# A gated unit's down projection in seven block products for the second half of the tokens, with weight combinations made beside the up products and up sums kept in PSUM

## The chip, the cores and the metric

The kernel runs on one core of a Trainium2 chip. Its metric is the device time of one launch, in microseconds (us). Engines are named as in the profile: PE is TensorE's matmul and PEld its weight load, DVE is VectorE, ACT is ScalarE, POOL is GpSimd, SP is SyncE, which here only issues DMAs.

## The reference

Input is x of 2048 tokens by 640. A state-space convolution comes first and is untouched here; then comes a gated unit without nonlinearity:

```python
x = x + ga * _A_ref(h, ...)                  # state-space convolution, by FFT
h = _layernorm(x, axis=-1) * (1 + cb) + sb
g = einsum("bsd,df->bsf", h, w_gate)         # 2048 x 640 by 640 x 1536
u = einsum("bsd,df->bsf", h, w_up)
x = x + gb * einsum("bsf,fd->bsd", g * u, w_down)   # 2048 x 1536 by 1536 x 640
```

All data are fp32.

## The kernel before

The gated unit begins about 519 us into the program and runs in two halves of 1024 tokens. A half has two token blocks tb of 512. In each half an up stage makes h = g * u, transposed (features on partitions, 512 tokens on the free axis), and a down stage multiplies it with w_down and adds the residual.

Every factor of a matmul is split into hi and lo parts of type fp32r: `hilo` has ACT write a rounded copy and DVE subtract it from the original. A product is three matmuls: hi by hi, lo by hi, hi by lo. `prod` issues them for a list of blocks of the contraction axis.

**Up stage.** The features F = 1536 are NF = 12 blocks of 128; block i counts through both halves (0 to 23). Tokens (the two blocks of 512), the contraction axis and the pair of gate and up weights make a two by two block product, which is done by seven products of blocks for eight (Winograd's form), with the fifth 128 of the contraction axis apart. For each i: `sums_u` (POOL) builds weight differences in tf, `split_u` splits them into wth/wtl and wsuh/wsul, `split_g` splits the gate weights into wsgh/wsgl. `x_1` and `x_2` (15 matmuls of 512 columns) multiply the gate weights with the first tokens; `y_1`, `z_1`, `y_2`, `z_2`, `y_3` (39 matmuls) are the other products. Each of these seven products has a PSUM bank of its own, from six banks pa0 to pa5 in turn, and the partial sums are added in SBUF: S6, S67 and c by DVE, ZT and the final product by POOL. x_1 and x_2 run AHEAD = 4 blocks ahead. The token combinations (`s_sums`, `s_split`, `s_one`, `s_five`) stand at the start of a half.

**Down stage.** For each tb, `down(tb, f)` runs over the 12 blocks f, four groups t of 128 tokens, three hi/lo terms and two column pieces (C0 = 384 and the other 256 of the 640 columns). h is the stationary factor, w_down (already times gb; `fold` makes it in the first half, on POOL, and keeps it in DRAM as wdg) the moving one. `d_prep` splits one block of h and one of weights, LEAD = 3 blocks ahead. `fin` adds the residual and stores. During the first half's down stage the list `LATER` prepares the second half's tokens.

**Order and queues.** Each engine works off its instructions in the order in which the program emits them (`tc.manual_schedule`), so the loop at the end of the program is the schedule. All loads of this part are issued by SP, in program order: `raw` loads pairs of gate or down weights into wga (two buffers), `raw_u` gate and up weights into wgb and wur, `res_l` the residual rows.

Of the kernel before, what the change touches and what calls it, by code (L numbers as in the profile page):

```python
# [224 lines left out]
def tile_kernel(ctx: ExitStack, tc: tile.TileContext, I, out):  # L225
# [762 lines left out]
    LEFT = {"wga", "wgb", "wur", "xb0", "xb1", "hh1", "hl1", "a5", "a6", "a7", "a8", "a9", "wsgh", "wsgl", "e"}  # L988

    PAIRS = []  # L990
    for h in range(2):
        PAIRS += [("g", h * NF + 2 * p) for p in range(NF // 2)]
        PAIRS += [("d", 2 * h + T, 2 * p) for T in range(2) for p in range(NF // 2)]

    def raw():

        k = PAIRS.pop(0)
        t = mk("wga", [P, 2 * D], F32, 2)
        f = k[-1] % NF
# [8 lines left out]
        for j in range(2):  # L1008
            WR[(*k[:-1], k[-1] + j)] = w[j]
# [45 lines left out]
    def prod(ps, ks):  # L1055

        for n, (a, b) in enumerate(((0, 0), (1, 0), (0, 1))):
            for m, (w, k, x, l) in enumerate(ks):
                PE.matmul(ps, w[a][:, k], x[b][:, l], start=n == 0 and m == 0, stop=n == 2 and m == len(ks) - 1)  # L1059

    BANK = [0]

    def pa(j=None):

        if j is None:
            j = BANK[0]
            BANK[0] += 1
        return ps_a.tile([P, 512], F32, name=f"pa{j % 6}")

    def x_e(i):  # L1070
        UE[i] = mk("e", [P, 512], F32, 4)
        act(UE[i], UX.pop(i))

    def x_c(i):
        V.tensor_tensor(a_tile(i % NF), UX.pop(i), UE[i], op=OP.add)
# [25 lines left out]
    def head_st(tb):  # L1101
        if tb == 1:
            return a_tile(TV0 + NB - 1)[:, : 24 * NB].rearrange("p (i k s) -> p i k s", i=4, k=NB)
        return wp.tile([P, 4, NB, 6], F32, name="st0")
# [197 lines left out]
    for t in range(3 * NK + 24):  # L1302
# [17 lines left out]
        if t == 3 * NK + 1:  # L1320
# [3 lines left out]
            wp = ctx.enter_context(tc.tile_pool(name="wp", bufs=1, reuse_waits="tile"))  # L1324
            wdg = dram1.tile([P, NF, D], F32, name="wdg")
            wv = [I[n].rearrange("(k p) f -> p k f", p=P) for n in ("B_w_gate", "B_w_up", "B_w_down")]
# [19 lines left out]
    TMP = ("s6", "z", "s67")  # L1346
# [20 lines left out]
    def s_sums(k, E=G):  # L1367
# [3 lines left out]
        s4 = tmp(TMP[1 + k])  # L1371
# [20 lines left out]
    ZT, S6, S67 = {}, {}, {}  # L1392

    def y_1(i):
        ps = pa()
# [256 lines left out]
```

## Time and profile before

| | us |
|---|---|
| median of 3 runs | 1001.46 (999.91 to 1002.73) |
| the profiled execution | 1001.29 |
| its span, first to last instruction | 999.2 |
| PE busy in the span | 900.0 (90%) |
| DVE, POOL, ACT busy | 762.8, 564.3, 561.9 |

Busy time of PE is modelled from pipelined matmuls; the distance from one matmul to the next is shorter than the duration in a row. A row of a view by line or tile gives a name as output<-inputs; the helper `hilo` puts all its operations on two lines (L230 for ACT, L1024 for DVE), so they are told apart by tile. A wait in brackets is the idle time of the engine ahead of an instruction and what ended it.

### The profile page before, as it was taken

What the parts mean: (1) busy time and instruction counts of PE and PEld (TensorE: products, weight loads), DVE (VectorE), ACT (ScalarE), POOL (GpSimd) and SP (SyncE); (2) the same over time, 40 slices, a digit from 0 to 9 for tenths busy, and PEclk for the clock granted to TensorE, in tenths of its full rate; (3) what the DMA queues carried; (4) which work ended last, traced back from release to release, by engine and by line L of the source; (5) the groups of instructions that cost most, each with busy time, mean ns of one, the idle gap of its engine ahead of it and who ended that gap; (6) DMA issues with size and microseconds to landing.
All of it is one profiled execution on the core that took longest, in us unless ns stands there. A gap on an engine that the chain in (4) does not pass through costs nothing.

```text
span 999.2 us, 26832 instructions
## 1 busy us (share of the span) xinstructions
PE 900.0 (90%) x11192; PEld 727.2 (73%) x11192; DVE 762.8 (76%) x1399; ACT 561.9 (56%) x1048; POOL 564.3 (56%) x415
## 2 busy tenths in 40 slices
PE   4867898899789689998888999999999999999998
PEld 3565556675576467776555888879998888889998
DVE  8798569889979997975769788777576887768452
ACT  4869989987878979752354323235463422223331
POOL 5978899799789899930032667650112365542000
PEclk9877889999899899999999999999999999999999
DMA  8728754555256454577673442535635232212341
GB/s 265 254 50 301 227 176 135 194 163 167 68 163 202 129 161 120 164 248 214 210 210 123 153 150 87 184 132 159 209 134 202 88 105 80 79 53 59 100 159 53
DMA packets 147817, 153.16 MB, mean 153 GB/s; under 512 B 9200, under 2 KB 125424, under 8 KB 146288
## 3 DMA queue, kind: packets, MB, share of 16 engines
q1 hardware_dynamic: 145968, 148.43, 46.8%
q10 hardware_dynamic: 1728, 3.02, 0.8%
q8 instruction: 88, 1.44, 0.6%
q14 instruction: 33, 0.27, 0.1%
HBM read 110.45 MB, written 40.96 MB: 152 GB/s over the span
## 4 chain that ended last, share of the span: by engine, by line
PE 63%; DVE 16%; ACT 10%; issue 4%; DMA 4%; POOL 2%; SPq 1%; DVEq 0%; ACTq 0%; POOLq 0%
PE pa L1059 26%; PE pa L1463 16%; PE kg L807 2%; DMA xsb<-A_u 2%; PE kg L822 2%; PE psfc L889 2%; ACT L230 1%; PE psfb L889 1%; PE psfa L889 1%; PE psfc L946 1%; PE psfb L946 1%; PE psfa L946 1%; PE psfc L868 1%; ACT trb L230 1%; PE psfa L844 1%
## 5 line engine op out<-in xcount | busy, mean ns | idle before, releaser
L710 POOL TENSOR_TENSOR EQ<-LQ,RH 128x1536 f32<-128x1536 f32 x40 | 124.2, 3105 | 9.9 <-DVE QtB L767 9.7
L230 ACT ACTIVATE z<-pa 128x512 f32<-128x512 f32 x24 | 14.4, 598 | 175.7 <-POOL a L1430 112.1
L1024 DVE TENSOR_TENSOR wsgl<-wga,wsgh 128x640 fp32r<-128x640 f32 x72 | 70.0, 976 | 46.1 <-ACT wsgh L230 46.1
L1412 POOL TENSOR_TENSOR z<-z,s 128x512 f32<-128x512 f32 x24 | 32.1, 1337 | 126.5 <-DVE s L1411 72.0
L230 ACT ACTIVATE wsgh<-wga 128x640 fp32r<-128x640 f32 x72 | 52.5, 732 | 65.1 <-PE pa L1463 47.9
L1024 DVE TENSOR_TENSOR wtl<-tf,wth 128x256 fp32r<-128x256 f32 (+1 forms) x72 | 42.7, 594 | 48.3 <-ACT wth L230 48.3
L1463 PE MATMUL pa<-wsgh,sh 128*128 128x384 f32 (+1 forms) x304 | 69.4, 309 | 0.0
L1463 PE MATMUL pa<-wsgh,sl 128*128 128x384 f32 (+1 forms) x304 | 69.0, 308 | 0.0
L1463 PE MATMUL pa<-wsgl,sh 128*128 128x384 f32 (+1 forms) x304 | 69.0, 308 | 0.0
L710 POOL TENSOR_TENSOR Phb<-LH,DH 128x1536 int32<-128x1536 int32 x20 | 62.3, 3115 | 11.2 <-ACT tra L230 11.2
L710 POOL TENSOR_TENSOR EP<-LP,RH 128x768 f32<-128x768 f32 x40 | 66.1, 1651 | 0.0
L710 POOL TENSOR_TENSOR Pha<-LH,DH 128x1536 int32<-128x1536 int32 (+1 forms) x21 | 62.5, 2974 | 2.2 <-ACT trb L230 1.9
L1036 POOL TENSOR_TENSOR tf<-wur,wgb 128x256 f32<-128x256 f32 x23 | 17.8, 776 | 75.6 <-DVE wtl L1024 50.0
L822 PE MATMUL kg<-QtB,PtB 64*32 64x64 f32 x2560 | 48.7, 229 | 5.4 <-DVE QtB L766 5.3
L822 PEld LDWEIGHTS kg<-QtB,PtB 64*32 64x32 f32 x2560 | 41.6, 114 | 15.4 <-issue 6.5
L1463 PEld LDWEIGHTS pa<-wsgh,sl 128*128 128x128 f32 x304 | 46.4, 187 | 0.0
L1463 PEld LDWEIGHTS pa<-wsgl,sh 128*128 128x128 f32 x304 | 46.3, 187 | 0.0
L1059 PE MATMUL pa<-sh,wtl 128*128 128x512 f32 x144 | 45.0, 394 | 1.4 <-DVE wtl L1024 1.2
L1463 PEld LDWEIGHTS pa<-wsgh,sh 128*128 128x128 f32 x304 | 46.3, 187 | 0.0
L1059 PE MATMUL pa<-sh,wth 128*128 128x512 f32 x144 | 44.9, 393 | 0.5 <-ACT wth L230 0.5
L1059 PE MATMUL pa<-sl,wth 128*128 128x512 f32 x144 | 44.5, 390 | 0.0
L1430 POOL TENSOR_TENSOR a<-s,z 128x512 f32<-128x512 f32 x24 | 38.8, 1618 | 5.4 <-DVE s L1429 5.4
(604 smaller groups left out, 2925.2 us busy)
## 6 DMA issues: line engine op xcount, KB each, us to landing
wga<-wdg SPq DMA_DIRECT2D x24, 640.0 KB, 5.0
wga<-B_w_gate SPq DMA_DIRECT2D x12, 640.0 KB, 5.9
wgb<-B_w_gate SPq DMA_DIRECT2D x24, 320.0 KB, 3.4
wur<-B_w_up SPq DMA_DIRECT2D x24, 320.0 KB, 4.0
xb<-x2d SPq DMA_DIRECT2D x6, 1280.0 KB, 5.7
TVb<-WD SPq DMA_DIRECT2D x22, 256.0 KB, 3.6
t_tw<-w_mod SPq DMA_DIRECT2D x3, 1600.0 KB, 8.5
t_ti<-w_mod SPq DMA_DIRECT2D x3, 1600.0 KB, 7.9
```

The costliest lines, as they stand in the source:

```text
L230: return S.activation(o, i, f, **kw)
L710: G.tensor_tensor(o.rearrange("p x (h l) -> p x h l", l=8), lo.unsqueeze(2).to_broadcast([P, rows, nh, 8]), hi.rearrange("p h x -> p x h") ...
L807: PE.matmul(kg[j * 32 : j * 32 + 32, dd, :], PtA[:, c, dl * 4 + j, :], QtA[:, c, dl * 4 + j, :], start=dd == 0 and c == 0, stop=False, til ...
L822: PE.matmul(kg[j * 32 : j * 32 + 32, dd, :], PtB[lo : lo + 64, c, r, :], QtB[lo : lo + 64, c, r, :], start=False, stop=dd == 7 and c == 1, ...
L889: PE.matmul(r[c][par * 64 : par * 64 + 64, i, :], t_tw[:, k0 + k, c, :], src[:, k, :], start=True, stop=True, tile_position=(0, par * 64))
L946: PE.matmul(r[par][:, i], t_ti[lo : lo + 64, qd * 4 + i, c, :], x[lo : lo + 64, c, i, :], start=c == 0, stop=c == 1, tile_position=(lo, 0))
L1024: V.tensor_tensor(lo, v, hi, op=OP.subtract)
L1036: E.tensor_tensor(t[:, 0:2], u[:, 0:2], g[:, 0:2], op=OP.subtract)
L1059: PE.matmul(ps, w[a][:, k], x[b][:, l], start=n == 0 and m == 0, stop=n == 2 and m == len(ks) - 1)
L1412: G.tensor_tensor(ZT[i], ZT[i], S67[i], op=OP.add)
L1430: G.tensor_tensor(a_tile(NF + i % NF), c, ZT.pop(i), op=OP.mult)
L1463: PE.matmul(ACC[tb][t][c], x[:, ts], w[:, cs], start=st, stop=f == NF - 1 and n == 2 and (c == 0 or t % 2 == 1))
```

## The change

1. **The second half's down stage** is a two by two block product too: the two token blocks (tb 2 and 3) by two halves of the features (NH = 6 blocks each) by two halves of the columns (DC = 320), done by seven products j of six blocks c each; step m = 6 j + c. `d_sum` (DVE) makes sums and differences of blocks of h, `d_prep(m)` splits one block of them, LEAD = 5 steps ahead. `down(half, m)` has 4 x 3 matmuls of 320 columns. The products are added in PSUM in two sets of four banks, A (j = 0, 2, 4, 6) and C (j = 1, 3, 5), and `post` adds a set to the right quarter of the residual after each product. The last product runs token group by token group. The first half keeps its form under the names `p_prep` and `plain`.
2. **The weight combinations** for the seven products are made during the second half's up stage, three groups of four blocks (r): `f_load` loads from wdg, `f_sum` (DVE) makes four differences, `f_hi` (ACT) and `f_lo` (DVE) split seven tiles, which ACT and SP store to DRAM (wdc). The dictionary FOLD says at which third of which block. `w_load` (issued by POOL) loads them back, 640 KB each, for two steps.
3. **Up sums kept in PSUM.** x_1, y_1, y_2 and y_3 of a block add to one bank (pa0 to pa4 in turn), z_1 and z_2 to another (`cbank`: pa5 and the two psg banks). The sums in between are read out of the bank as it stands: S6 by ACT after y_1, ZT by ACT after z_1, ZT plus the bank by DVE after y_2. For blocks 0 and 1, whose x_1 product was made before, DVE adds UE. The final products are made by DVE.
4. **Split gate weights are stored.** `keep` (SP) stores the hi and lo parts of the first half to DRAM (wsd), and the second half's `split_g` loads them back by a DMA that POOL issues. `raw` no longer loads for the second half.
5. The prologue of the first half is in another order and includes x_1 and x_2 of block 4.

The core of the diff; unchanged bodies, renamings of buffers and the list of tiles are left out.

```diff
+    def wsg():
+        return mk("wsg", [P, 2, D], F32R, 4)
+
     def split_g(i):
-        WS[i] = mk("wsgh", [P, NB, P], F32R, 4), mk("wsgl", [P, NB, P], F32R, 4)
+        t = wsg()
+        WS[i] = tuple(t[:, j].rearrange("p (k m) -> p k m", k=NB) for j in range(2))
+        if i >= NF:
+            G.dma_start(t, wsd[:, i - NF])
+            return
         hilo(*WS[i], WR.pop(("g", i)))
         if i > 3:
+            keep(i, t)
             used(i)
+        else:
+            WK[i] = t
+            if i == 1:
+                raw()
+
+    WK = {}
+
+    def keep(i, t):
+        SY.dma_start(wsd[:, i], t.bitcast(F32))
...
-    def prod(ps, ks):
+    def prod(ps, ks, first=True, last=True):
 
         for n, (a, b) in enumerate(((0, 0), (1, 0), (0, 1))):
             for m, (w, k, x, l) in enumerate(ks):
-                PE.matmul(ps, w[a][:, k], x[b][:, l], start=n == 0 and m == 0, stop=n == 2 and m == len(ks) - 1)
-
...
+                PE.matmul(ps, w[a][:, k], x[b][:, l], start=first and n == 0 and m == 0, stop=n == 2 and m == len(ks) - 1, skip_group_check=True)
+
+    def pa(j):
+        return ps_a.tile([P, 512], F32, name=f"pa{j}")
+
+    def pg():
+        return ps_g.tile([P, 512], F32, name="psg")
+
+    CB = [0]
+
+    def cbank():
+
+        j = CB[0]
+        CB[0] += 1
+        return pg() if j % 3 else pa(5)
...
     def x_1(i):
-        UX[i] = pa()
-        prod(UX[i], [(WS[i], k, HX[0], k) for k in (0, 1)])
+        UX[i] = UA[i] = pa(i % 5)
+        prod(UX[i], [(WS[i], k, HX[0], k) for k in (0, 1)], last=False)
         x_e(i)
 
     def x_2(i, c=True):
-        UX[i] = pa()
+        UX[i] = cbank()
         prod(UX[i], [(WS[i], k, HX[0], k) for k in (2, 3, 4)])
         WS.pop(i)
...
     def y_1(i):
-        ps = pa()
-        prod(ps, [(WT[i], 2 + k, HX[2], 2 + k) for k in range(2)])
-        S6[i] = tmp("s6")
-        V.tensor_tensor(S6[i], ps, UE[i], op=OP.add)
+        if i < 2:
+            UA[i] = pa(i)
+        prod(UA[i], [(WT[i], 2 + k, HX[2], 2 + k) for k in range(2)], i < 2, False)
+        S6[i] = mk("a23", [P, 512]) if i % 2 == 0 else tmp("s6")
+        if i < 2:
+            V.tensor_tensor(S6[i], UA[i], UE[i], op=OP.add)
+        else:
+            act(S6[i], UA[i])
 
     def z_1(i):
-        ps = pa()
-        prod(ps, [(WT[i], k, HX[2], k) for k in range(2)] + [(WU[i], 2, HX[1], 2)])
+        UC[i] = cbank()
+        prod(UC[i], [(WT[i], k, HX[2], k) for k in range(2)] + [(WU[i], 2, HX[1], 2)], last=False)
         ZT[i] = tmp("z")
-        act(ZT[i], ps)
+        if i < 2:
+            V.tensor_tensor(ZT[i], UC[i], UE[i], op=OP.add)
+        else:
+            act(ZT[i], UC[i])
 
     def y_2(i):
-        ps = pa()
-        prod(ps, [(WT[i], 4 + k, HX[2], 4 + k) for k in range(2)])
-        S67[i] = tmp("s67")
-        V.tensor_tensor(S67[i], ps, S6[i], op=OP.add)
-        V.tensor_tensor(S6[i], ZT[i], S6[i], op=OP.add)
-        G.tensor_tensor(ZT[i], ZT[i], S67[i], op=OP.add)
+        prod(UA[i], [(WT[i], 4 + k, HX[2], 4 + k) for k in range(2)], False, False)
+        V.tensor_tensor(ZT[i], UA[i], ZT[i], op=OP.add)
 
     def z_2(i):
-        ps = pa()
-        prod(ps, [(WU[i], k, HX[2], 6 + k) for k in range(3)])
+        prod(UC[i], [(WU[i], k, HX[2], 6 + k) for k in range(3)], False)
         c = S6.pop(i)
-        V.tensor_tensor(c, ps, c, op=OP.add)
-        if i == 0:
-            x_c(0)
-            x_c(1)
+        V.tensor_tensor(c, UC.pop(i), c, op=OP.add)
+        SC[i] = c
+
+    SC = {}
+
+    def y_3(i):
+        prod(UA[i], [(WT[i], 6 + k, HX[1], k) for k in range(2)] + [(WU[i], 3, HX[1], 2)], False)
+        h = a_tile(NF + i % NF)
+        if i < 2:
+            V.tensor_tensor(UE[i], UA.pop(i), UE[i], op=OP.add)
+            V.tensor_tensor(h, UE.pop(i), ZT.pop(i), op=OP.mult)
+        else:
+            V.tensor_tensor(h, UA.pop(i), ZT.pop(i), op=OP.mult)
         a = AT[i % NF]
-        V.tensor_tensor(a, a, c, op=OP.mult)
-
-    def y_3(i):
-        ps = pa()
-        prod(ps, [(WT[i], 6 + k, HX[1], k) for k in range(2)] + [(WU[i], 3, HX[1], 2)])
-        c = S67.pop(i)
-        V.tensor_tensor(c, ps, c, op=OP.add)
-        G.tensor_tensor(a_tile(NF + i % NF), c, ZT.pop(i), op=OP.mult)
-
-    C0 = 384
-    ACC, AH, WD2, AR = {}, {}, {}, {}
-
-    def d_prep(tb, f):
+        V.tensor_tensor(a, a, SC.pop(i), op=OP.mult)
...
+    def d_prep(m):
+        j, c = divmod(m, NH)
+        v = S1[c] if j == 3 else AT[(0, NH, 0, 0, NF, NH, NF + NH)[j] + c]
+        AH[m] = d_pair(m)
+        hilo(*AH[m], v)
...
+    def d_sum(j, c, E=G):
+
+        a, b = AT[c], AT[NF + c]
+        if j == 0:
+            if c == 0:
+                HQ[0], HQ[1] = (mk(n, [P, NB, 512], F32R) for n in ("hh1", "hl1"))
+            S1[c] = (HQ[0][:, c].bitcast(F32) if c < NB else tmp("s6"))
+            E.tensor_tensor(S1[c], b, AT[NF + NH + c], op=OP.add)
+            E.tensor_tensor(b, a, b, op=OP.subtract)
+        elif j == 1:
+            E.tensor_tensor(a, S1[c], a, op=OP.subtract)
+        else:
+            E.tensor_tensor(AT[NH + c], AT[NH + c], a, op=OP.subtract)
+
+    def w_load(q):
+        WD[q] = wsg()
+        G.dma_start(WD[q], wdc[:, q // 3, q % 3])
+
+    def down(half, m, last=False):
+        j, c = divmod(m, NH)
+        if c == 0:
+            if j == 0:
+                ACC["A"] = [pa(t) for t in range(4)]
+            if j in (1, 3):
+                ACC["C"] = [pa(4), pa(5), pg(), pg()]
+        ps = ACC["AC"[j in (1, 3, 5)]]
+        w = [WD[m // 2][:, l, c % 2 * DC : c % 2 * DC + DC] for l in range(2)]
+        for t in range(4) if not last else (last - 1,):
+            for n, (a, b) in enumerate(((0, 0), (1, 0), (0, 1))):
+                PE.matmul(ps[t][:, :DC], AH[m][a][:, t * P : t * P + P], w[b], start=c == 0 and n == 0 and j in (0, 1, 3), stop=c == NH - 1 and n == 2, skip_group_check=True)
...
+    POST = ((0, 0), (0, 0), (0, 1), (1, 1), (1, 1), (0, 1), (1, 0))
+
+    def post(half, j, ts=range(4), E=None):
+
+        r, c = POST[j]
+        x = XQ[r, c]
+        ps = ACC["AC"[j in (1, 3, 5)]]
+        for t in ts:
+            V.tensor_tensor(x[:, t], ps[t][:, :DC], x[:, t], op=OP.add)
...
+    def f_sum(n):
...
+
+    FH = {}
+
+    def f_hi(r, j, n):
+        FH[j] = mk("hst", [P, D], F32R) if n % 2 else FT["t"][:, 3].bitcast(F32R)
+        act(FH[j].rearrange("p (k d) -> p k d", k=2), FT["v"][j])
+        S.dma_start(wdc[:, j, r, 0], FH[j].bitcast(F32))
+
+    def f_lo(r, j):
+        v = FT["v"][j]
+        V.tensor_tensor(v.bitcast(F32R), v, FH.pop(j).rearrange("p (k d) -> p k d", k=2), op=OP.subtract)
+        SY.dma_start(wdc[:, j, r, 1].rearrange("p (k d) -> p k d", k=2), v)
...
+    FOLD = {n: [] for n in range(80)}
+    for r in range(3):
+        b = (1, 13, 25)[r]
+        for n in range(4):
+            FOLD[b + 1 + n // 2].append((f_sum, n))
+        for j in range(7):
+            o = b + 3 + j + (max(j - 1, 0) if r == 2 else 0)
+            FOLD[o].append((f_hi, r, j, j))
+            FOLD[o + 1].insert(0, (f_lo, r, j))
+        if r < 2:
+            FOLD[b + 10].append((f_load, r + 1))
...
+            for i in range(2):
+                x_c(i)
             for k in (0, 2, 1, 3, 4):
                 tokens2(1, 1, k, False)
-            for i in (2, 3):
-                x_1(i)
-                x_2(i, False)
             sums_u(0)
-            for k in range(2):
-                s_sums(k, V)
+            s_sums(0, V)
+            x_1(2)
+            x_2(2, False)
+            s_sums(1, V)
             for k in range(2):
                 s_split(k, 2)
+            x_1(3)
+            x_2(3, False)
             split_u(0, "a")
+            x_c(2)
+            for j in range(4):
+                keep(j, WK.pop(j))
+            split_g(4)
+            x_1(4)
+            x_2(4, False)
+            x_c(3)
             for k in range(2):
                 s_split(k, 1)
             s_one(4)
             split_u(0, "b")
             for k in range(2):
                 s_split(k, 3)
-            x_c(2)
             split_u(0, "c")
             for k in (2, 3):
                 s_one(k)
             s_five(V)
-            x_c(3)
             for k in range(2):
                 s_split(k, 4)
-            sums_u(1, V)
-            raw()
+            x_c(4)
             raw_u(2)
             need(1, "gbd")
             gbr = mk("gbr", [P, D])
             SY.dma_start(gbr, gbd)
             res_l(0, 1)
         else:
+            f_load(0)
             for j in range(AHEAD):
-                if LEAD <= j + 1 < AHEAD:
+                if LEAD0 <= j + 1 < AHEAD:
                     split_g(i0 + j + 1)
                 x_1(i0 + j)
                 x_2(i0 + j)
             for k in (2, 3):
                 s_one(k)
             raw_u(i0 + 2)
-            res_l(2, 0)
-            res_l(3, 1)
         for f in range(NF):
             i = i0 + f
+            late = 1 - half < f <= NF - AHEAD
             y_1(i)
-            z_1(i)
-            late = 0 < f <= NF - AHEAD
+            if i == 0:
+                sums_u(1, V)
             if late:
                 x_1(i + AHEAD - 1)
+            z_1(i)
+            if half:
+                combos(3 * f)
             if f + 1 < NF:
                 split_u(i + 1, "a")
             y_2(i)
             if f + 1 < NF:
                 split_u(i + 1, "bc")
-            if f + AHEAD < NF:
+            if 1 - half <= f + half and f + AHEAD < NF:
                 split_g(i + AHEAD)
             if f + 2 < NF:
                 sums_u(i + 2)
                 raw_u(i + 3)
             if late:
                 x_2(i + AHEAD - 1)
+            z_2(i)
+            if half:
+                combos(3 * f + 1)
+            if half and f >= NF - 2:
+                d_prep(2 * (f - NF + 2))
             y_3(i)
-            z_2(i)
             if half == 0:
                 fold(f)
+                if f >= NF - 2:
+                    p_prep(0, f - NF + 2)
+                continue
+            combos(3 * f + 2)
+            if f >= NF - 3:
+                for c in (0, 1) if f == NF - 3 else (f - NF + 4,):
+                    d_sum(0, c, V if half else G)
+                w_load(f - NF + 3)
             if f >= NF - 2:
-                d_prep(2 * half, f - NF + 2)
...
+                d_prep(2 * (f - NF + 2) + 1)
+            if f == NF - 3:
+                xq_l(half, 0, 0, 0)
+                xq_l(half, 0, 1, 1)
+        if half == 0:
+            for T in range(2):
+                for f in range(NF):
+                    for n in (2, 3) if T == f == 0 else (f + LEAD0,):
+                        if n < NF:
+                            p_prep(T, n)
+                        elif T == 0:
+                            p_prep(1, n - NF)
+                        else:
+                            split_g(n)
+                    plain(T, f)
+                    if f == NF - 1:
+                        fin(T)
+                    for g_, *a_ in LATER.get((T, f), ()):
+                        g_(*a_)
+            continue
+        w_load(3)
+        todo = list(SUMS)
+        for m in range(7 * NH):
+            j, c = divmod(m, NH)
+            for n in range(4, 1 + LEAD) if m == 0 else (m + LEAD,):
+                if n < 7 * NH:
+                    d_prep(n)
+            if m % 2 == 0 and m and m // 2 + 3 < 21:
+                w_load(m // 2 + 3)
+            if todo and m > 0:
+                d_sum(*todo.pop(0), V)
+            if j < 6:
+                down(half, m)
+            if c == 0 and j:
+                post(half, j - 1)
+                if j == 2:
+                    xq_l(half, 1, 1, 0)
+                if j == 5:
+                    xq_l(half, 1, 0, 0)
+            combos(36 + m)
+        for t in range(4):
+            for m in range(6 * NH, 7 * NH):
+                down(half, m, t + 1)
+            post(half, 6, (t,), (SY, S)[t % 2])
```

More of the change, by code (lines that the diff above doesn't have):

```diff
@@ L987, in tile_kernel @@
     TV0, TV1 = 5, 10
[L988 to L993, printed above, removed]
+    LEFT = {"wga0", "wga1", "wgb", "wur", "xb0", "xb1", "hh1", "hl1", "a5", "a6", "a7", "a8", "a9", "wsg", "hst", "e"}
+    PAIRS = [("g", 2 * p) for p in range(NF // 2)] + [("d", T, 2 * p) for T in range(2) for p in range(NF // 2)]
+    NP = len(PAIRS)
     def raw():
+        t = mk(f"wga{(NP - len(PAIRS)) % 2}", [P, 2 * D])
         k = PAIRS.pop(0)
-        t = mk("wga", [P, 2 * D], F32, 2)
-        f = k[-1] % NF
+        f = k[-1]
         if k[0] == "g":
@@ L1473, in fin @@
             x = XR[tb][:, t, :]
[L1474 to L1484 removed]
+            V.tensor_tensor(x[:, :C0], AC[tb][t][0], x[:, :C0], op=OP.add)
```

142 lines of the change are left out of this document (81 added, 61 removed).

## The prediction

> **What bounds the kernel now.** I read the page first, then the chain of waits in order of time from 519 us on (where the gated unit begins), then the busy time of the engines by stage, and last the single rows that price an operation. Everything ahead of the gated unit is the same in both kernels, but for one load that is issued a little earlier.
>
> ```profile
> span 999.2 us, 26832 instructions
> PE 900.0 (90%) x11192; PEld 727.2 (73%) x11192; DVE 762.8 (76%) x1399; ACT 561.9 (56%) x1048; POOL 564.3 (56%) x415
> ```
>
> ```profile
> 537.56 1.28 DVE sl L1024 x2
> ...
> 544.52 103.91 PE pa L1059 x451
> ...
> 758.89 1.92 DVE wsgl L1024
> 761.34 149.04 PE pa L1059 x648
> 910.38 84.62 PE pa L1463 x576
> ```
>
> The chain gives start, length and owner of each piece. In the second half it is TensorE alone: 149.04 us of up products (L1059) and 84.62 us of down products (L1463), with no other engine in between. So there the time goes down exactly as TensorE's work does, until another engine falls behind. The stages, with the count of TensorE's instructions:
>
> ```profile
> 520.60:668.40 147.80, 144.92 (x622) 115.05 (x621) 121.33 (x175) 49.74 (x111) 84.59 (x74) 1.00 0.42 140
> 668.40:759.80 91.40, 89.81 (x617) 88.75 (x615) 64.83 (x138) 48.75 (x80) 17.30 (x15) 1.00 0.46 153
> 761.30:910.20 148.90, 148.86 (x648) 121.63 (x649) 109.88 (x165) 46.27 (x102) 67.03 (x63) 1.00 0.31 98
> 910.20:995.10 84.90, 84.78 (x577) 84.39 (x575) 40.47 (x63) 26.83 (x44) 1.44 (x2) 1.00 0.31 98
> 883.70:910.20 26.50, 26.50 (x118) 21.96 (x117) 19.41 (x29) 8.04 (x18) 12.49 (x12) 1.00 0.15 47
> ```
>
> Columns: length, then busy time (and count) of PE, PEld, DVE, ACT and POOL, the granted clock, the DMA engines' share, GB/s. The rows are first-half up, first-half down, second-half up, second-half down, and the last three blocks of the second-half up. One up product takes 149.04 / 648 = 0.230 us, one down product 84.62 / 576 = 0.147 us. The first-half up has 618 up products (its 622 hold four transposes): 618 x 0.230 = 142.1 of 147.8 us, so 5.7 us are idle there, nearly all before the chain's long TensorE piece at 544.52. VectorE is the second engine, 110 of 149 us in the second-half up.
>
> **The second-half down products.** Before: 12 blocks x 4 token groups x 3 hi/lo terms x 2 column pieces (384 and 256) = 576 matmuls, 184,320 columns. After: 7 products x 6 blocks x 4 x 3 = 504 matmuls of 320 columns, 161,280 columns. The mean width is 320 in both, so the mean spacing of 0.147 us carries over, whether columns or the number of matmuls and weight loads set it: 504 x 84.62 / 576 = 74.0 us, **10.6 us less**. By columns alone it is 84.62 x 161,280 / 184,320, again 74.0. The Trainium skill (TensorE: Matmul & The Clock Gate, part 1, "Wait — 56ns, not 53.3ns?") gives a spacing of N / 2.4 GHz plus 2.5 ns; by that page 72 matmuls fewer of 136 ns would be 9.8 us, an estimate, and the trace's 147 ns is the one I use.
>
> **VectorE and GpSimd in the up blocks.** Partial sums now stay in PSUM. Per block VectorE's seven operations on products become five (L1411 goes, L1398 becomes a ScalarE copy, L1429's add becomes the product that GpSimd made), and GpSimd's two 128x512 operations go. The price of VectorE's other rows hangs on those two:
>
> ```profile
> 852.49 0.43 DVE L1024 TENSOR_TENSOR wtl<-tf,wth 128x256 fp32r<-128x256 f32 x1 [3.17 <-ACT wth L230]
> 852.93 0.69 DVE L1410 TENSOR_TENSOR s<-pa,s 128x512 f32<-128x512 f32 x1
> 854.26 0.42 DVE L1024 TENSOR_TENSOR wtl<-tf,wth 128x256 fp32r<-128x256 f32 x1
> 854.60 1.65 DVE L1024 TENSOR_TENSOR wsul<-wur,wsuh 128x384 fp32r<-128x384 f32 x1
> 856.17 0.68 DVE L1024 TENSOR_TENSOR wtl<-tf,wth 128x512 fp32r<-128x512 f32 x1
> 856.77 0.28 DVE L1024 TENSOR_TENSOR wsul<-wgb,wsuh 128x128 fp32r<-128x128 f32 x1
> ...
> 854.49 1.34 POOL L1412 TENSOR_TENSOR z<-z,s 128x512 f32<-128x512 f32 x1 [4.81 <-ACT wsgh L230]
> ...
> L1024 DVE TENSOR_TENSOR wsul<-wur,wsuh x24: 551/1650/1653, 530.7 to 900.4; 128x384 fp32r<-128x384 f32 x24
> L1024 DVE TENSOR_TENSOR wsgl<-wga,wsgh x68: 811/826/1921, 545.2 to 981.5; 128x640 fp32r<-128x640 f32 x68
> L1024 DVE TENSOR_TENSOR sl<-a,sh x50: 673/685/1327, 527.0 to 968.1; 128x512 fp32r<-128x512 f32 x50
> L1423 DVE TENSOR_TENSOR a<-a,s x24: 694/734/1289, 548.3 to 911.7; 128x512 f32<-128x512 f32 x24
> ...
> L230 ACT ACTIVATE z<-pa x24: 597/598/599, 538.3 to 905.0; 128x512 f32<-128x512 f32 x24
> L230 ACT ACTIVATE wsgh<-wga x68: 718/731/742, 541.4 to 980.7; 128x640 fp32r<-128x640 f32 x68
> ```
>
> The wsul row takes 1.65 us while a GpSimd add runs beside it and 0.55 (its minimum) alone; wsgl and sl range from 0.81 to 1.92 and from 0.67 to 1.33. (The Trainium skill, SBUF — State Buffer, "Who interferes with whom", has VectorE with two SBUF inputs contend with a GpSimd read; the row agrees.) Without the two I take the low values. A block then costs VectorE 3 x 0.69 (as L1410) + 0.73 = 2.8 for its sums and products and 0.42 + 0.42 + 0.55 + 0.68 + 0.28 = 2.35 for splitting the weights, 5.1 us in all, plus 0.69 for x_c where there is an x product. The weight combinations (4 differences and 7 lo parts per group of four blocks, at 0.82) add 9.0 / 4 = 2.3 us. That is 8.1 us in a block of 54 x 0.230 = 12.4 us: TensorE stays the bound, and this costs nothing. ScalarE was busy 46 of 149 us, 3.9 a block; it gains a copy (0.6) and 7 / 4 hi parts (1.3) and loses the gate weights' split (0.73): 5.1 of 12.4.
>
> The last three blocks have no x product: 39 matmuls, 8.8 us each. There VectorE has 2.8 + 2.35 + 2.5 (three combinations) + 4 x 0.69 (d_sum) = 10.4 us, then 2.8 + 2.35 + 1.6 + 1.4 (d_sum) + 1.4 (two d_prep) = 9.6, then 2.8 + 0.8 + 1.4 + 1.4 = 6.4: 26.4 against TensorE's 26.5. The order matters: y_3 of a block may not add to its bank before VectorE has read it after y_2, and that read stands behind the combinations of the block before. Laid out in order, it comes 0.2 us late in the second of the three. If the remaining GpSimd sums (tf) slow VectorE as above, it is some 3 us. I take **+0.5**, bounds 0 and 3.4.
>
> In the down stage VectorE has per step of 12 x 0.147 = 1.76 us one lo part (0.68), in steps 1 to 14 one or two sums (0.69 each), and every six steps four additions of 320 columns (about 0.48 each, between the next two rows): 38 x 0.68 + 16 x 0.69 + 28 x 0.48 + 2 x 0.82 = 52 of 74 us. LEAD is 5 steps, 8.8 us; laid out step by step the worst backlog, around step 12, is 5 us. So **0**.
>
> ```profile
> L1475 DVE TENSOR_TENSOR xb<-pa,xb 128x384 f32<-128x384 f32 x16 | 8.8, 549 | 9.8 <-PE pa L1463 9.8
> L1478 DVE TENSOR_TENSOR xb<-pa,xb 128x256 f32<-128x256 f32 x16 | 6.7, 418 | 0.9 <-PE pa L1463 0.7
> ```
>
> **The two joints of half 0 and its start.**
>
> ```profile
> 671.85 0.39 PE L1463 MATMUL pa<-wsgh,e 128*128 128x256 f32 x1 [1.36 <-DVE s L1418]
> ...
> 761.34 0.73 PE L1059 MATMUL pa<-hh,wsgh 128*128 128x512 f32 x2 [1.55 <-DVE xb L1475]
> ...
> 538.76 0.42 DVE L1036 TENSOR_TENSOR tf<-wur,wgb 128x256 f32<-128x256 f32 x1
> ```
>
> At 671.85 the first down product waits for the bank that z_2 wrote last. The new bank order puts the banks of earlier blocks first and that of y_3 last, 2.6 us into the stage: **-1.4**. At 761.34 the second half waits for the first addition of fin, which stands behind a weight split of 1.92 us (758.89 in the chain). That split is gone (the stored hi and lo are loaded back), so fin can begin before TensorE ends: **-1.5**. What hides the load is 10.5 us of down products between its issue and its use (three blocks of 24 x 0.147 us).
>
> At the start x_1(4) and x_2(4) (15 products, 3.5 us) come ahead of block 0. But y_2(0) now adds to the bank that VectorE must first copy (S6), and this copy stands in VectorE's queue behind the prologue's last lo part, which ended at 538.84 before, is now one split later (0.4, as some idle time takes part of it), and behind x_c(4): 539.2 + 0.7 + 0.7 = 540.6. Then four differences of 0.42 and ZT's 0.7: z_2(0) starts at about 543.0, and blocks z_2(0), y_3(0) end at 547.1. By then 30 + 15 + 39 = 84 matmuls are done since 520.67, 19.3 us of work: 7.1 us idle against 5.7 before. **+1.4**, bounds -2 and +4. Four stores of 640 KB are issued by SP ahead of it; they read tiles written long before.
>
> **The loads and the end.**
>
> ```profile
> wga<-wdg SPq DMA_DIRECT2D x24, 640.0 KB, 5.0
> xb<-x2d SPq DMA_DIRECT2D x6, 1280.0 KB, 5.7
> ...
> DMA to landing us min/median/max: 4.0/5.0/6.7
> ...
> 994.70 0.28 PE L1463 MATMUL pa<-wsgl,hh 128*128 128x256 f32 x1
> ...
> 995.82 0.41 DVE L1478 TENSOR_TENSOR xb<-pa,xb 128x256 f32<-128x256 f32 x1
> ```
>
> The 21 combined weight tiles of 640 KB now come by DMAs that GpSimd issues, one per two steps (3.5 us), each when its tile is free, 6 steps (10.6 us) ahead of use. No row here shows a load issued by GpSimd; the nearest is SP's at 5.0 us. The last load has less room, since the last product runs token group by token group: issued at step 34, needed 5.3 us later. With the rows' 4.0 to 6.7 us that is 0 to 1.4 us: **+0.5**. SP's stores and loads of a block roughly double DMA traffic in the second half from 98 GB/s at a share of 0.31, which leaves room; GpSimd's sums (tf) queue behind its load of gate weights, which waits for a tile that is free by then.
>
> At the end the last addition began 1.1 us after the last matmul did, 0.8 us after its end, behind others. Now it is one of 320 columns for a token group that took 18 x 0.147 = 2.6 us: **-0.6**.
>
> **Sum:** -10.6 - 1.4 - 1.5 - 0.6 + 1.4 + 0.5 + 0.5 = -11.7 us. The profiled execution took 1001.29 us (span 999.2 and 2.1 around it), the median of the runs is 1001.46. 1001.3 - 11.7 = **989.6 us**.
>
> **Rivals.** *A: the loads from GpSimd run one after another.* With a landing of T each and no overlap, the last of 18 lands at 18 T and 8.8 us of products follow; at T = 5.0 the stage takes 98.8 instead of 74.0 us, and the kernel 989.6 + 24.8 = 1014 us. It starts to cost above 3.6 us a load and ends slower than before above 4.3 us. For it: 5.0 is the only price of this size. Against it: twice the bytes land in 5.7 us, so most of the 5.0 is no transfer, and nothing makes these loads wait for each other, as each has its own tile. (The Trainium skill, DMA: Bandwidth & Descriptors, "Anatomy of one DMA", fits 2.0 us plus bytes / 436e3 for GpSimd's loads, 3.5 us here by that page, just under the point; no run here shows it yet.) Chance 0.10. *B: VectorE keeps its slow prices* (tf's sums, or the new loads, in place of the adds): 3 us more in the last three blocks and 3 at the start, 995 us. For it: tf's sums remain on GpSimd. Chance 0.17. *C: the kept banks bind in every block:* each add to a bank waits for its reader, and 0.4 us lost in each of 22 blocks and joints uses up 9 to 11 us, 999 to 1001 us, no change that can be measured. Against it: z_1's 2.0 us lie between y_1 and y_2, a copy takes 0.6; x_2 and z_2, 4.1 us, lie ahead of y_3. Chance 0.06. *D: a stall that I did not see*, a store that holds up SP's queue in front of the block loads: slower by some us, 0.05.
>
> **The numbers.** The forecast has the rest, 0.62. The lowest sum of the bounds (start -2, no other loss) is 985. The range goes from 984.5 through B and C to 1001: A and D are left out. A measurement here tells 0.3%, 3 us, from no change. Faster is the forecast and B, 0.62 + 0.17 = 0.79; same is C, 0.06; slower is A and D, 0.10 + 0.05 = 0.15.
>
> **What would show it.** In the profile after: 504 matmuls of 128x320 in one chain piece of about 74 us; up blocks of 12.4 us in the second half; wsul near 0.55 and no GpSimd add of 128x512 in the blocks; no wait at the two joints; a wait for VectorE's copy of S6 at about 540. Wrong would be: TensorE waiting for a load of wsg (A), second-half up over 152 us (B or C), or a spacing of the 320-column matmuls away from 0.147 us.

## The result, and the profile after

The changed kernel takes 995.19 us (median of 4 runs, 994.1 to 996.17), the kernel before beside it 1000.98 (4 runs, 999.91 to 1002.73): a ratio of 0.994, interval 0.992 to 0.9961. A second comparison, further down, gave 992.87 against 1001.24, 0.9928 (0.9903 to 0.9953). The change makes the kernel faster, by 5.8 us in the first comparison and 8.4 in the second, and not by 11.7.

The profiled execution took 996.15 us with a span of 994.4. First its page's head and two groups of its DMA part (queue, count, KB of one, median us from issue to landing):

```profile
span 994.4 us, 26747 instructions
wsg<-wdc POOLq DMA_DIRECT2D x21, 640.0 KB, 5.1
wsg<-wsd POOLq DMA_DIRECT2D x12, 640.0 KB, 4.7
```

The engines by stage, in the columns of the prediction's table: first-half up, first-half down, second-half up, second-half down.

```profile
526.30:677.20 150.90, 144.23 (x622) 117.67 (x620) 92.09 (x157) 56.63 (x121) 53.34 (x52) 0.98 0.56 189
677.20:766.30 89.10, 89.10 (x617) 88.83 (x617) 61.78 (x137) 45.46 (x75) 14.64 (x15) 1.00 0.47 150
766.30:915.50 149.20, 148.80 (x650) 121.52 (x649) 99.87 (x169) 61.91 (x126) 40.25 (x54) 1.00 0.69 227
915.50:991.00 75.50, 74.43 (x505) 73.89 (x504) 50.06 (x90) 22.38 (x38) 8.99 (x17) 1.00 0.74 228
```

The down stage of the second half has one matmul in eight less and is shorter by 9.4 us. The first half's down stage has no idle time left. The first-half up stage is longer, at a mean clock of 0.98 instead of 1.00.

The exact first starts of each stage in the two traces give the balance. "Start" is counted from the eighth ScalarE copy `Wb<-psfc` of the stages ahead (475.80 us before, 478.07 after) to the gated unit's first product `x_1(2)`; the tail is what follows the start of the last matmul.

| stage | before | after | difference | predicted |
|---|---|---|---|---|
| start | 44.87 | 48.33 | +3.46 | 0 |
| first-half up | 147.72 | 150.85 | +3.13 | +1.4 |
| first-half down, with both joints | 92.95 | 89.11 | -3.84 | -2.9 |
| second-half up | 148.88 | 149.21 | +0.33 | +0.5 |
| second-half down | 84.49 | 75.12 | -9.37 | -10.6 + 0.5 |
| tail | 4.48 | 3.70 | -0.78 | -0.6 |
| sum | 523.39 | 516.32 | -7.07 | -11.7 |

The remaining 2.3 us arise ahead of the start, in stages of the same program text. In the eleven traces of this study that same point lies anywhere between 473.1 and 480.4 us, and two traces of the changed kernel have it at 478.07 and 475.58; so I read the kernels by stage and take the 2.3 us for scatter.

**The start.** SP's queue ahead of the gated unit, first in the profile of before, then of after (start, us of issue, what is loaded):

```profile
488.07 0.91 SPq L959 DMA_DIRECT2D TVa<-WD  x2
489.02 0.51 SPq L961 DMA_DIRECT2D xsb<-A_u  x1
```

```profile
491.93 0.37 SPq L1000 DMA_DIRECT2D wga<-B_w_gate  x1
492.47 0.95 SPq L959 DMA_DIRECT2D TVa<-WD  x2
493.47 0.51 SPq L961 DMA_DIRECT2D xsb<-A_u  x1
```

SP's wait ahead of the early load (engine waited for, us in total, times, longest) and VectorE in the profile of after at that time:

```profile
SPq L1000 <- DVE wsg L1022: 8.5, 1, 8.5
```

```profile
487.85 2.60 DVE L1130 BATCH_NORM_STATS2 a<-xb 128x6 f32<-128x128 f32 x13
490.37 2.28 DVE L1022 TENSOR_TENSOR wsg<-wga,wsg 128x640 fp32r<-128x640 f32 x3
```

`raw()`, which loads gate and up weights into wga, is now called at the end of `split_g(1)`. Its load may start only when VectorE's split has read wga, and that split stands behind 13 statistics operations; SP waits 8.5 us for it. SP works its queue in order, so TVa and xsb, which the stage ahead needs at once, are issued 14.4 us behind the Wb copy (492.47) instead of 12.3 (488.07).

**The start of half 0.** TensorE in the profile of after, and the VectorE operations that it waits for:

```profile
540.80 0.39 PE L1074 MATMUL pa<-hl,wsuh 128*128 128x512 f32 x1
547.33 1.19 PE L1074 MATMUL pa<-sh,wth 128*128 128x512 f32 x2 [6.13 <-DVE a L1423]
548.32 1.05 PE L1074 MATMUL pa<-sh,wtl 128*128 128x512 f32 x2
```

```profile
545.29 0.69 DVE L1022 TENSOR_TENSOR sl<-a,sh 128x512 fp32r<-128x512 f32 x1
545.89 0.69 DVE L1095 TENSOR_TENSOR a<-psg,a 128x512 f32<-128x512 f32 x1
546.50 0.68 DVE L1423 TENSOR_TENSOR a<-pa,e 128x512 f32<-128x512 f32 x1
```

`y_2(0)` waits for the copy of S6 (L1423), behind the last lo part and `x_c(4)`: the predicted mechanism. The copy ends 20.8 us behind the first product (547.18 - 526.39) where 19.9 was worked out (540.6 - 520.67). What was not worked out stands in the windows of this place:

```profile
541.00:545.00 4.00, 0.19 (x1) 0.00 (x0) 3.31 (x7) 1.99 (x4) 0.00 (x0) 1.00 0.53 155
545.50:552.00 6.50, 4.67 (x11) 3.76 (x12) 5.78 (x13) 1.86 (x5) 0.00 (x0) 0.50 0.67 241
552.50:556.00 3.50, 3.50 (x17) 2.89 (x16) 1.43 (x3) 0.82 (x3) 2.86 (x4) 1.00 0.59 175
```

From 545.3 to 552.1 us the granted clock is half: 11 products follow each other at 0.427 us instead of 0.227, which is 2.2 us. Before, TensorE is idle for 2.9 us in this stage (147.80 us less 144.92 busy), in short pieces and at a clock of 1.00. The longest piece is this one:

```profile
544.52 0.50 PE L1059 MATMUL pa<-hh,wsul 128*128 128x512 f32 x1 [0.83 <-DVE wsul L1024]
```

**The end of the loads.** TensorE in the last stage of after: the one wait there is for the last combined weight tile.

```profile
979.81 1.05 PE L1560 MATMUL pa<-wsg,a 128*128 128x320 f32 x6
981.92 0.39 PE L1560 MATMUL pa<-wsg,hh 128*128 128x320 f32 x1 [1.06 <-DMA wsg<-wdc]
```

### The profile page after: what moved, and what is told of

Same layout as the page of the kernel before. It is cut to its first block, busy times and chain, and to the rows that moved or that the text cites. A ratio compares the mean times of both kernels' runs of the same rounds, so it can differ in the third digit from the quotient of the medians.

```text
span 994.4 us, 26747 instructions
## 1 busy us (share of the span) xinstructions
PE 893.7 (90%) x11120; PEld 725.3 (73%) x11120; DVE 729.1 (73%) x1408; ACT 577.0 (58%) x1071; POOL 510.8 (51%) x400
## 4 chain that ended last, share of the span: by engine, by line
PE 55%; DVE 14%; ACT 12%; issue 10%; DMA 6%; POOL 2%; SPq 1%; DVEq 0%; POOLq 0%; ACTq 0%
PE pa L1074 17%; PE pa L1508 9%; PE psg L1074 8%; PE psfc L889 2%; PE kg L822 2%; PE kg L807 2%; PE psfa L889 2%; ACT L230 1%; PE psfb L889 1%; ACT trb L230 1%; DMA TVa<-WD 1%; PE psfb L946 1%; PE pa L1560 1%; ACT tra L230 1%; PE psfc L946 1%
## 5 line engine op out<-in xcount | busy, mean ns | idle before, releaser
L1508 PE MATMUL pa<-wsg,sh 128*128 128x384 f32 (+1 forms) x304 | 58.6, 311 | 0.0
L1508 PEld LDWEIGHTS pa<-wsg,sh 128*128 128x128 f32 x304 | 45.8, 189 | 0.0
L1547 POOL DMA_DIRECT2D wsg<-wdc x21 | 11.2, 532 | 66.5 <-PE pa L1560 35.5
L1022 DVE TENSOR_TENSOR wsg<-wga,wsg 128x640 fp32r<-128x640 f32 x36 | 32.9, 920 | 11.9 <-ACT wsg L230 11.9
L1022 DVE TENSOR_TENSOR sl<-a,sh 128x512 fp32r<-128x512 f32 x53 | 36.7, 712 | 5.8 <-ACT sh L230 5.8
L230 ACT ACTIVATE sh<-a 128x512 fp32r<-128x512 f32 x53 | 32.0, 622 | 14.9 <-PE psg L1560 6.2
L230 ACT ACTIVATE wsg<-wga 128x640 fp32r<-128x640 f32 x36 | 26.1, 729 | 21.7 <-PE pa L1508 11.0
L230 ACT ACTIVATE wth<-tf 128x256 fp32r<-128x256 f32 (+1 forms) x72 | 32.2, 479 | 9.8 <-PE pa L1074 5.3
L1074 PE MATMUL pa<-hh,wsg 128*128 128x512 f32 x136 | 36.7, 395 | 0.5 <-DVE wsg L1022 0.5
L765 DVE TENSOR_TENSOR QtA<-tra,EQ 128x1024 f32<-128x1024 f32 x20 | 24.4, 1221 | 14.8 <-PE kg L807 9.2
```

Of the source, the lines that this page charges most:

```text
L230: return S.activation(o, i, f, **kw)
L765: return [lambda: V.tensor_tensor(Qt[:, :, :, 0:32], tr[:, :, :, ::-1], e[:, :, 0:32].unsqueeze(1).to_broadcast([P, 2, R, 32]), op=OP.mult ...
L1022: V.tensor_tensor(lo, v, hi, op=OP.subtract)
L1074: PE.matmul(ps, w[a][:, k], x[b][:, l], start=first and n == 0 and m == 0, stop=n == 2 and m == len(ks) - 1, skip_group_check=True)
L1508: PE.matmul(AC[tb][t][c], x[:, ts], w[:, cs], start=st, stop=f == NF - 1 and n == 2 and (c == 0 or t % 2 == 1))
L1547: G.dma_start(WD[q], wdc[:, q // 3, q % 3])
```

## The experiments

Stage times are given as in the table above, from one trace of each kernel. The time of a whole run scatters by some us, the stages behind the start much less where the text is the same: the first-half up stage of the changed kernel by 0.7 (150.68 to 151.37), the others by 0.4 at most, but for the last stage of e1.

### e1: the early load back in its old place

The first place of the edit is `split_g`, the second the start of the gated unit. In the kernel before the call stands later in the program, at the end of the preparation, but SP has no other DMA in between: in SP's queue the load is back in its old place, behind the last store of the stage ahead.

```diff
-            if i == 1:
-                raw()
...
             new_h2()
+            raw()
```

> The changed kernel with its third early weight load (wga<-B_w_gate, L1000) issued at the start of the gated unit's code, as the kernel before has it, instead of straight after the second split. Theory (the load waits for the tile's split on VectorE and holds up the loads behind it in SP's queue): the gated unit's first up product starts 3.4 us earlier than in the changed kernel, and the time falls by 3.4 us, to about 991.8 (range 990.5 to 993). Rival (the 3.4 us is drift of the stages ahead, of run or of placement): no change, 995.2 within 1.

988.56 us (6 runs, 987.19 to 991.61), 0.9875 of the kernel before (0.9846 to 0.9904): below the range that was expected. The start takes 43.57 us for 48.33, the other stages are within 0.4 of the changed kernel but for the last, 76.20 for 75.12. SP's queue stands again as before:

```profile
485.34 0.91 SPq L959 DMA_DIRECT2D TVa<-WD  x2
486.29 0.51 SPq L961 DMA_DIRECT2D xsb<-A_u  x1
```

TVa is issued 12.3 us behind the Wb copy (473.08), and 4.8 us come back, more than the 3.4 expected. The wait for the last weight tile grew to 2.14 us, as that load took 6.89 us to land where it took 5.81 in the changed kernel; why it did is open.

```profile
973.58 0.39 PE L1558 MATMUL pa<-wsg,hh 128*128 128x320 f32 x1 [2.14 <-DMA wsg<-wdc]
```

### e2: the early load alone, in the kernel before

```diff
+        elif i == 1:
+            raw()
...
-            raw()
```

> The kernel before with that one load moved as the change moves it, and nothing else of the change. Theory (queue): the gated unit's first up product starts 3.4 us later than in the kernel before, and the time rises by 3.4 us, to about 1004.4 (range 1003 to 1006). Rival (it comes from something else of the change, or from drift): 1001 within 1.

1004.64 us (12 runs, 1000.97 to 1007.06) against 1002.33 (17 runs), ratio 1.0017 (0.9998 to 1.0037). The interval just reaches no change; the trace shows the place. The start takes 47.21 us for 44.87, TVa is issued 14.4 us behind the Wb copy as in the changed kernel, and the other stages differ from before by 0.33 at most. So the move costs the kernel before 2.3 us with nothing else of the change present, less than the 3.4 expected.

Over all traces, the start takes 46.7 to 48.3 us in the seven with the early load (mean 47.5) and 43.6 to 46.1 in the four with the late one (mean 44.7). The move costs **2.8 us**, with a scatter of one trace of some 1 us; the ranges do not overlap. The 3.46 of the first pair of traces held some of that scatter.

### e3: the idle time filled

```diff
             z_1(i)
+            if i == 0:
+                fill = pg()
+                for _ in range(24):
+                    PE.matmul(fill, WT[0][0][:, 2], HX[2][0][:, 2], start=True, stop=True)
```

> The changed kernel with 24 products of 512 columns, whose result nobody reads, put between z_1(0) and y_2(0), where TensorE idles for 6.1 us; they take 24 x 0.227 = 5.4 us. Theory (the idle itself lowers the granted clock afterwards): the clock stays at 1.00 behind that place, the 11 products at 0.427 us go at 0.227, and the time falls by 2.2 us, to 993.0 (range 992 to 994). Rival (the clock falls for another reason, or the cost lies in the wait alone): 995.2 or up to 1 us more.

The first-half up stage takes 149.33 us for 150.85, the stages behind it are as before the edit; the time is 992.52 us (6 runs, 991.39 to 996.5). TensorE at that place:

```profile
543.25 1.52 PE L1752 MATMUL psg<-sh,wth 128*128 128x512 f32 x6
545.46 0.70 PE L1074 MATMUL pa<-sh,wth 128*128 128x512 f32 x2 [0.68 <-DVE a L1423]
545.99 0.62 PE L1074 MATMUL pa<-sh,wtl 128*128 128x512 f32 x2
546.45 0.61 PE L1074 MATMUL pa<-sl,wth 128*128 128x512 f32 x2
547.52 0.93 PE L1074 MATMUL pa<-sh,wsuh 128*128 128x512 f32 x3 [0.46 <-DVE z L1432]
```

The 24 products do no work for the output, and the stage is shorter with them: the products behind them are at full speed, and `y_2(0)` starts 21.0 us behind the first product as it did without them (20.9). Of the 2.2 us 1.5 come back; part of the rest is the next wait, for VectorE's ZT (0.46 us), which the slow products had covered.

### e5: block 0 pulled into the preparation

```diff
             split_u(0, "b")
+            y_1(0)
             for k in range(2):
                 s_split(k, 3)
             split_u(0, "c")
-            for k in (2, 3):
-                s_one(k)
             s_five(V)
             for k in range(2):
                 s_split(k, 4)
+            z_1(0)
+            y_2(0)
+            for k in (2, 3):
+                s_one(k)
             x_c(4)
...
```

The loop over the blocks then leaves these three calls out for block 0.

> The changed kernel with y_1, z_1 and y_2 of block 0 written inside the preparation of half 0, so that VectorE's copy of S6 comes ahead of eight lo parts and the fifth difference; nothing is added or left out. Theory (the wait for the copy is a matter of VectorE's order; broken into pieces under 3 us the idle leaves the clock alone): y_2(0) starts some 5 us earlier, no product at 0.427 us is left, and the first half's up products take 147.9 us for 150.85 (range 146.9 to 149.4), the kernel 3.0 us less than 995.2. Rival (VectorE's sum of work is the bound there in any order): z_2, y_3 and the next block wait for the same total, only the clock's 1.5 to 2.2 us come back, 148.6 to 149.4.

992.02 us (6 runs, 990.23 to 994.38); the first-half up stage takes 148.34 us for 150.85, a gain of 2.5, between the two theories' values and in the theory's range. The wait for the S6 copy is gone and `y_2(0)` starts almost at once, but the next wait, of `z_2(0)` for VectorE's ZT behind a difference and three lo parts, is 2.9 us long, in TensorE's timeline:

```profile
539.14 0.73 PE L1074 MATMUL pa<-sh,wtl 128*128 128x512 f32 x2 [0.39 <-DVE wtl L1022]
539.71 0.62 PE L1074 MATMUL pa<-sl,wth 128*128 128x512 f32 x2
543.23 0.94 PE L1074 MATMUL pa<-sh,wsuh 128*128 128x512 f32 x3 [2.90 <-DVE z L1432]
```

Order gave back a part, VectorE's queue keeps the rest: from 540.6 us to the copy that `y_2(1)` waits for (552.2) it is busy for 11.44 of 11.61 us. And the clock was halved again, from 544.1 to 547.5 us, 0.9 us after TensorE had started anew: an idle of 2.9 us can do it too, against what I had expected. It cost nothing here, as e7 shows: the same order there, at full clock, takes the same 148.34 us.

### e6: the last product's order

```diff
-            if j < 6:
+            if m < 40:
...
-            for m in range(6 * NH, 7 * NH):
+            for m in (40, 41):
```

> The changed kernel with the seventh block product of the last stage taken in the order of the other six for its steps m = 36 to 39, and only its last two steps (m = 40, 41) group by group. Theory (the 1.06 us wait in the last stage is the first group's walk through all six weight tiles in 6 x 3 matmuls, faster than the last of the loads lands): that wait goes and the time falls by 1.1 us, to 994.1 (range 993.5 to 994.6), with the end behind the last matmul no longer. Rival (the last load binds in any order, or the closing of the groups becomes the tail): no change within 0.5.

The last stage takes 73.79 us for 75.12, the tail 3.69 as before the edit: 1.3 us less, the wait is gone. The time of 993.05 us (6 runs, 988.31 to 997.29) scatters too widely to show it; the trace does. 84.49 - 73.79 = 10.7 us is then the worth of the seven products by themselves.

### e7 and e8: the three mends together, and the fifth difference on GpSimd

> The changed kernel with three edits together: the third early weight load back at the start of the gated unit, block 0 pulled into the preparation, and the last block product's first four steps in the usual order. If they are independent: gated unit's start 43.6 us behind the last Wb copy (48.3 in the changed kernel), first up products 147.9, last stage 73.8; in sum 4.7 + 3.0 + 1.3 = 9.0 us less than the changed kernel's 995.2, 986.2 (range 983.5 to 989). Rival (the earlier start makes the last loads late again): last stage at 75 to 76, about 988.

988.25 us (4 runs, 987.01 to 988.54), 0.9874 of the kernel before (0.9854 to 0.9894). Last stage 73.79 as expected, with no wait for the last load, so the rival is out although its 988 is the time that came. First-half up 148.34, 0.4 above the expected 147.9, but just what e5 took; the start 46.13, 2.5 more than in e1, which is the scatter above. e8 is e7 with one more edit:

```diff
-            s_five(V)
+            s_five(G)
```

> The kernel of the three mends with the fifth difference (one subtraction of 128 by 512, 0.69 us on VectorE) given to GpSimd, which does nothing in the first 25 us of half 0. Theory (VectorE's sum of work is the bound in block 0): the first up products fall by 0.7 us, from 148.3 to 147.6 (range 147.0 to 147.9), most of it in the 2.9 us wait ahead of z_2(0). Rival (the wait is for another lo part, or GpSimd's subtraction ends too late): no change within 0.3. The gated unit's start, with the third load late, takes 43.6 to 46.2, some 2.6 us less than in the changed kernel beside it.

984.52 us (4 runs, 984.4 to 987.0), ratio 0.9841 (0.9818 to 0.9863): the fastest version of this study, 16.7 us ahead of the kernel before beside it. But the first-half up stage took 148.03 us, 0.3 less than e7 and outside the range given. The reason is in the rows of e7, then of e8, at the start of the half:

```profile
524.74 0.69 DVE L1393 TENSOR_TENSOR a<-a,a 128x512 f32<-128x512 f32 x1
```

```profile
523.41 1.73 POOL L1410 TENSOR_TENSOR s<-a,a 128x512 f32<-128x512 f32 x1 [8.97 <-DVE a L1395]
523.90 1.78 DVE L1393 TENSOR_TENSOR a<-a,a 128x512 f32<-128x512 f32 x1
```

GpSimd's subtraction runs beside one of VectorE's, which takes 1.78 us for 0.69: 1.1 us are lost. Off VectorE's queue come the subtraction and a wait of 0.70 us behind it, 1.4 us together. So VectorE is ahead by 0.3 us, and this is what the stage gained, since `y_2(1)` waits for VectorE in both kernels:

```profile
551.69 0.70 PE L1072 MATMUL pa<-sh,wth 128*128 128x512 f32 x2 [2.06 <-DVE s L1421]
```

```profile
550.57 0.70 PE L1072 MATMUL pa<-sh,wth 128*128 128x512 f32 x2 [0.44 <-DVE s L1421]
```

The wait ahead of `z_2(0)` fell from 2.89 to 1.51 us, and the clock was halved behind it. The windows of e7, then of e8, around that wait:

```profile
538.50:541.90 3.40, 0.52 (x3) 0.11 (x2) 2.60 (x6) 2.71 (x5) 0.00 (x0) 1.00 0.80 221
541.90:545.30 3.40, 3.39 (x15) 2.85 (x16) 3.37 (x7) 0.12 (x1) 0.00 (x0) 1.00 0.92 345
```

```profile
537.56:540.96 3.40, 1.48 (x6) 0.89 (x6) 3.30 (x7) 1.45 (x3) 0.00 (x0) 1.00 0.42 124
540.96:544.37 3.41, 3.41 (x9) 2.64 (x9) 3.38 (x8) 0.32 (x1) 0.00 (x0) 0.50 1.01 321
```

The shorter idle was followed by half speed (9 products in the next window), the longer one was not (15). The slow products only filled time that TensorE waits for VectorE otherwise (0.44 us ahead of `y_2(1)` instead of 2.06): from the hi and lo parts behind the fifth difference to the copy for `y_2(1)`, VectorE is busy for 11.43 of 11.60 us in e7 and 11.44 of 11.61 in e8.

### The changed kernel a second time

> The changed kernel again, beside e8 on one chip. It gives a second trace of the stages: if they are a matter of the program, first up products 150.8, first down 89.1, second up 149.2, second down 75.1 within 0.3 each, and all scatter of the time lies ahead of the gated unit, whose start takes 47.5 (46.5 to 48.5) behind the last Wb copy.

992.87 us (7 runs, 990.59 to 998.02). The start takes 47.68 us, in the bounds given; behind it 150.68, 89.13, 149.23 and 75.10 us repeat the first trace within 0.2, with the long idle and 6.8 us of half clock at the same place.

### e4: two of three terms in the last stage

```diff
+                if n == 2 and j < 6:
+                    continue
...
```

> The changed kernel with the hi-by-lo term left out of the first six block products of the last stage (144 of 504 matmuls), the loads unchanged. Theory (TensorE alone bounds the last stage): 144 x 0.147 = 21.2 us less, the stage takes 54 us for 75.1. Rival (the loads come next): the profile after shows 228 GB/s at a busy share of 0.74 in this stage; at full share the same bytes need 0.74 x 75.1 = 55.6 us at the least, and with 5.1 us from issue to landing behind each freed buffer more, 58 to 65.

978.3 us (2 runs). The last stage takes 64.14 us: 11.0 of the 21.2 us are saved. That is in the rival's range, but not for its reason. TensorE's waits in that stage (engine waited for, us in total, times, longest):

```profile
PE pa L1562 <- DVE sl L1022: 4.7, 5, 1.3
PE pa L1562 <- DMA wsg<-wdc: 1.7, 1, 1.7
PE pa L1562 <- DVE wga L1577: 0.3, 1, 0.3
```

VectorE's lo parts come next after TensorE, not the loads. The other 3.4 us between 64.1 and the 54 expected for TensorE alone are no wait in this view: a part is clock (0.97 in the stage; half from 953.00 to 956.41 us, where TensorE had been busy for 1.80 of the 3.41 us before), the rest I did not separate.

## Why the prediction was half right

- **The down products: right.** 504 matmuls at 0.147 us were to take 74.0 us; without the last wait they take 73.8 (e6), -10.7 for -10.6. VectorE's 52 us there were 50.06.
- **The end of the loads: right in kind, too small.** +0.5 was the value, 0 to 1.4 the bounds, and 1.06 came. The load landed in 5.81 us where the sum had 4.0 to 6.7.
- **The two joints: right,** -3.8 for -2.9 (the waits of 1.36 and 1.55 are gone, and some smaller ones).
- **VectorE in the up blocks: right in its prices, lucky in the +0.5.** wsul's median fell from 1.65 to 0.55 us with GpSimd's additions gone. The second-half up stage gave away 0.33 us for +0.5, but not in the last three blocks, where VectorE was thought to come late: TensorE's one wait in that stage is in its first block, for ScalarE's copy of S6.

```profile
L1022 DVE TENSOR_TENSOR wsul<-wur,wsuh x24: 550/552/554, 539.0 to 904.7; 128x384 fp32r<-128x384 f32 x24
...
783.95 0.73 PE L1074 MATMUL pa<-sh,wth 128*128 128x512 f32 x2 [0.36 <-ACT a L230]
```

- **Ahead of the gated unit: wrong.** The sentence "Everything ahead of the gated unit is the same in both kernels, but for one load that is issued a little earlier" costed that load at nothing. It costs 2.8 us over all traces (3.5 in the first pair), shown from both sides (e1 takes it out, e2 puts it in). What failed is the asking: the load's own wait was not looked up, nor who stands behind it in SP's queue. Rival D named a store that holds up SP's queue, but looked for it in front of the block loads.
- **The start of half 0: right wait, wrong price.** +1.4 was worked out from idle time alone, 7.1 us for 5.7. It was +3.1, since the idle, in one piece of 6.13 us, was followed by half clock for 11 products, a term that the sum did not have. e3 shows it: 1.5 us come back when TensorE is kept busy. The 5.7 is no idle time of the profile either: it is what the stage took beyond 618 x 0.230 us, of which the profile shows 2.9 as idle; the rest is in products that follow more slowly. Taken the same way, the changed kernel has 8.7 us, 2.2 of them clock and 6.5 the rest, so the term without the clock was +0.9 for +1.4. The bounds (-2 to +4) held it.
- **Rivals A, B and C:** A and B did not come. The measured 995.2 us is the 995 of B, but by chance: VectorE's low price held in all 24 rows above, and the second-half up took 149.2 us. Of C there is one wait of 0.36 us in the second half. The loads from GpSimd overlap: 5.1 us from issue to landing, above the 3.6 us from which A would cost, yet 21 of them cost one wait of 1.06 us. The Trainium skill (DMA: Bandwidth & Descriptors, "Anatomy of one DMA") would give 3.5 us for such a load, an estimate by its fit; this trace has 5.1.

The range (984.5 to 1001) held the time. The forecast was 5.6 us too low, of which the load (2.8 to 3.5) and the clock (1.5 to 2.2) make up most. By the stages it missed 4.6 us (7.07 for 11.7).

## What to carry to other kernels

When a DMA is issued earlier on a shared queue, look up what it must wait for: if its tile is still being read, everything behind it in the queue waits as well, and the loads that the current stage needs are the ones that pay. Order VectorE's queue by what TensorE needs first. A long idle of TensorE can cost more than itself, since the products after it may run at half speed: filling it gave 1.5 us back here, while breaking it into pieces of 2.9 us and less did not keep the clock up in two traces of three. Half speed cost nothing where TensorE had to wait for VectorE next (e5). Before an operation is given to GpSimd, look at what VectorE does beside it. Compare stages between traces, with a common mark, where whole runs scatter by more than the edit is worth.

## What the runs showed of the hardware

- **The clock falls in stretches of one length and not in order with the idle.** In the first half's up stage the halved stretches lasted 6.8 us (the five traces with the idle of 6.1 us) or 3.4 (e5, e8). An idle of 2.9 us was followed by no half clock in e7 and by 3.4 us of it in e5, and one of 1.51 us (with 0.41 just before it) by as much in e8. The Trainium skill (TensorE: Matmul & The Clock Gate, part 1) has a free-running window of about 3.4 us, and a fall to half after an idle one. The length agrees, and a window that runs free would explain why e5 and e7 differ. That a whole idle window is needed does not agree: in the 3.4 us ahead of the fall TensorE was busy for 1.48 us in e8 and for 1.80 in e4. Where the threshold lies stays open.
- **A subtraction moved to GpSimd cost VectorE more than it took there.** It takes 0.69 us on VectorE; on GpSimd it took 1.73, and a VectorE subtraction of the same size beside it took 1.78 us for 0.69 (e8 and e7).
